# Float64 weights narrowed on VectorE alone, with a new cost model and table of urgencies

## The chip, the cores and the metric

The kernel runs on one core of a Trainium2 chip. A core has five engines with a queue each: TensorE (PE: matmuls, with PEld for its weight loads), VectorE (DVE), ScalarE (ACT), GpSimd (POOL) and SyncE (SP), which here only issues DMAs. The metric is the device time of one execution in microseconds; lower is better.

## The reference, cut to what matters

```python
# attention, 4 x 8 heads, 576 positions, head size 64
q_d, k_d, v_d = means of 4 neighbouring positions          # 144 positions
out_up = repeat(softmax(q_d k_d^T / 8) v_d, 4)              # global part
scores = where(|i - j| < 4, q k^T / 8, -1e9)                # local part, a band
x = out_up + softmax(scores) v                              # -> [2304, 512]
# first feed-forward layer, weights are float64
x = ((x @ w_a) * (x @ w_b)) @ w_out                         # 512 -> 1536 -> 512
# second one, weights are float64, alpha float32
h = x @ w_in
return (max(h, 0) + alpha * min(h, 0)) @ w_out2             # 512 -> 2048 -> 512
```

The five weight matrices come as float64. The kernel reads each number as two 32-bit words and must make a float32 of them (its exponent scaled by a power of two) before it can be used.

## The kernel before, in words

All large products run on TensorE in float16, with each operand split into a high and a low half (`split`, line 413), so that a product is three matmuls. The work has these stages, and the names in the trace are those of the tiles:

- *Attention of batch b* (four batches, six tiles of 96 positions each). `turn` transposes q and k, `soft` makes the band's softmax, `p_turn` and `av_t` multiply with v; the global part is made by `g_top`, `g_minus`, `g_exp`, `g_out` and `od_turn`; `x_add` (line 703) adds the two and splits the sum into `xt`. `v_sum` (line 758) adds neighbouring rows of v on GpSimd, for batches 1 to 3.
- *Weights.* A piece is 1024 numbers a partition (`w_a`, `w_b`, `w_in2`) or 512 (`w_out`, `w_out2`). `narrow` (line 463) turns the two words of a number into one: ScalarE scales the low word into place, VectorE masks sign and top exponent bit as int16, VectorE shifts and masks the high word as int32, and GpSimd adds the two. Then ScalarE takes the sum of squares, and ScalarE and VectorE split the piece into two float16 halves. `wab_chunk`, `wo_words`, `wi_chunk` and `wo2_words` (lines 940 to 1006) call it, for 12, 12, 8 and 16 pieces. The raw pieces lie in a few buffers that are used in turn: the load of a later piece waits until `narrow` and what follows has read the buffer.
- *Main matmuls.* `s1(j, f)` makes 128 columns of the first hidden layer for 288 tokens (j = 0 to 7, f = 0 to 11; 24 matmuls, then two operations each on ScalarE and VectorE); `s2` multiplies with `w_out` and leaves `x2`; `s3` and `s4` are the second layer for blocks of 384 tokens. Blocks j = 0 and 1 are taken together, two f at a time, so that they follow the weights as these are narrowed; then s2 of block 0, s1 of block 2, and so on.

The order of the work is not written by hand. Every instruction goes through a planner (`Plan`, line 26): `cost` (line 93) gives its duration, `lat` (line 186) the delay from an engine to the next, and `reschedule` (line 201) plays the program through, always taking on each engine the ready operation with the highest priority. A priority is the length of work that follows, plus a bias, plus an urgency from the table `URGENT` (line 1259) that has an entry for each group of operations. The main matmuls are a chain whose order is fixed (`chain`, line 440): the planner may put other work between them but not swap them. `fill` (line 244) then puts matmuls on `idf`, which compute nothing, into the gaps that the plan leaves on TensorE between 4 and 200 us. The orders of the queues that come out are fixed in the program; on the chip each engine runs its queue in order and waits on semaphores.

Of the kernel before, what the change touches and what calls it, by code (L numbers as in the profile page):

```python
# [7 lines left out]
F32 = mybir.dt.float32  # L8
F16 = mybir.dt.float16
BF16 = mybir.dt.bfloat16  # L10
# [9 lines left out]

class Op:
    __slots__ = ("eng", "calls", "dur", "bias", "preds", "succ", "tail", "est", "left", "start", "end", "name", "dma",
                 "reads", "writes", "n", "free", "prio")


class Plan:
# [4 lines left out]
    def __init__(self, nc):  # L31
        self.nc = nc
        self.ops = []
        self.group = None
        self.live = {}
        self.bias = 0.0
        self.name = ""
        self.rel = 0.0

    @staticmethod  # L40
    def region(ap):
# [49 lines left out]
        return n  # L91

    def cost(self, eng, method, out, ins, kw):
        n = self.free(out)
        if eng == self.PE:
            if method == "transpose":
                n = self.free(out)
                w = 2 if ins[0].dtype == F32 else 1
            else:
                w = 4 if ins[0].dtype == F32 else 1  # L100
            return max(0.03, n * w * 0.000425)
        m = max([n] + [self.free(a) for a in ins])
        if eng == self.POOL:
            return 0.2 + m * (0.0026 if method == "tensor_tensor" else 0.0011)
        if eng == self.ACT:
            if ins and ins[0].dtype == U32:
                return 0.2 + 0.00095 * m
            return 0.2 + 0.0009 * m + (0.19 if kw.get("accum_out") is not None else 0)
        if out.dtype == I16:
            return 0.1 + 0.00144 * m  # L110
        if method in ("tensor_scalar", "tensor_copy", "memset", "tensor_scalar_mul"):
            return 0.12 + 0.0009 * m
        return 0.14 + 0.0011 * m

    def __call__(self, eng, method, *args, **kw):
        if "out" in kw:
            writes, ins = [kw["out"]], [a for a in args if hasattr(a, "ap")]
        else:
            writes, ins = [args[0]], [a for a in args[1:] if hasattr(a, "ap")]
        out = writes[0]  # L120
        for k, a in kw.items():
            if k == "accum_out":
                if a is not None:
                    writes.append(a)
            elif k != "out" and hasattr(a, "ap"):
                ins.append(a)
        o = self.group
        if o is None or eng != self.PE:
            o = self.new(eng)
        if eng == self.SP:  # L130
            el = kw["in_"]
            parts = [int(c) for _, c in el.ap]
            nb = SIZE[el.dtype]
            for c in parts:
                nb *= c
            run = min(min(int(x.ap[-1][1]) for x in (kw["out"], kw["in_"])) * SIZE[el.dtype], 4096)
            rate = 230e3 if run >= 1024 else 150e3
            o.dma = (nb / rate, 2.2)
            o.dur += 1.0
        else:  # L140
            o.dur += self.cost(eng, method, out, ins, kw)
# [13 lines left out]

    def new(self, eng):
        o = Op()
        o.eng, o.calls, o.dur, o.bias, o.name, o.dma = eng, [], 0.0, self.bias, self.name, None
        o.reads, o.writes, o.preds, o.succ, o.free = [], [], set(), [], self.rel
        return o  # L160

# [22 lines left out]
        o.reads = o.writes = None  # L184

    def lat(self, a, b):
        if a.eng == b.eng and not a.dma:
            return 0.0 if a.eng == self.PE else 0.06
        if a.eng == self.PE:
            return 0.3  # L190
        return 0.2

    def schedule(self, chain):
        for a, b in zip(chain, chain[1:]):
# [74 lines left out]
    def issue(self):  # L269
        for o in self.order:  # L270
            for f, args, kw in o.calls:
                f(*args, **kw)  # L272


LAST = None

# [2 lines left out]
def kernel(  # L279
# [136 lines left out]

    idf = const.tile([128, 128], F32, name="idf")
    ones = const.tile([2, 128], F32, name="ones")

    def top_of(m, n):  # L420

# [38 lines left out]
            return t[:, i + 1].rearrange("p a b c -> p (a b c)").bitcast(F32)  # L460
        return t[:, i + 1].rearrange("p a b -> p (a b)").bitcast(F32)

    def narrow(raw, dst):


        w = raw.bitcast(I32).rearrange("p (n t) -> p n t", t=2)
        h = raw.bitcast(I16).rearrange("p (n t) -> p n t", t=4)
        A("activation", out=w[:, :, 0], in_=raw.bitcast(U32).rearrange("p (n t) -> p n t", t=2)[:, :, 0],
          func=ACTF.Copy, scale=2.0 ** -29)
        V("tensor_scalar", out=h[:, :, 1], in0=h[:, :, 3], scalar1=-0x4000, scalar2=None, op0=ALU.bitwise_and)  # L470
        d = dst.bitcast(I32)
        V("tensor_scalar", out=d, in0=w[:, :, 1], scalar1=3, scalar2=0x3FFFFFFF,
          op0=ALU.logical_shift_left, op1=ALU.bitwise_and)
        G("tensor_tensor", out=d, in0=d, in1=w[:, :, 0], op=ALU.add)

    def cols_in(raw, w, c):
        dma(raw.rearrange("p (k f) -> p k f", k=KD), w[:, c * CW:(c + 1) * CW].rearrange("(k p) f -> p k f", p=128))
# [14 lines left out]
    def rows_in(i, w, raw):  # L492
        dma(raw, w[i * 128:(i + 1) * 128, :])

    def rows_narrow(t, i, n, raw):
        narrow(raw, slot(t, i))
        A("activation", out=raw.bitcast(BF16)[:, :DM], in_=slot(t, i), func=ACTF.Square, accum_out=row_ss[n][:, i:i + 1])

    def split_rows(t, i, rf):
# [12 lines left out]
              op=ALU.mult)  # L512
        return prep_rows(F1, fac, us_o)

    def cols_words(t, i, raw):
        narrow(raw, slot(t, i))

    def cols_bound(t, i0, c):
        m = c["m"] = ring("wm", [128, 2])
# [420 lines left out]
    def wab_chunk(c):  # L940
        st = {}
        for j in range(2):
            cols_words(wab, 2 * c + j, raws[(2 * c + j) % 3])
            wab_load(2 * c + j + 3)
        cols_bound(wab, 2 * c, st)
        cols_split(wab, 2 * c, us_ab, st)
# [7 lines left out]
        rows_in(i, w_out, wo_raw[i])  # L954

    def wo_words(i):
        rows_narrow(wo, i, F1, wo_raw[i])
        for n in {0: [5], 1: [6], 2: [7], 5: [8], 6: [9], 8: [10], 9: [11]}.get(i, []):
            wo_load(n)

# [31 lines left out]
    def wi_chunk(c):  # L992
        x = {}
        for j in range(2):
            cols_words(wi, 2 * c + j, raws2[(2 * c + j) % 4])
            wi_load(2 * c + j + 4)
        cols_bound(wi, 2 * c, x)
        cols_split(wi, 2 * c, us_i, x)
# [3 lines left out]
            rows_in(i, w_out2, xr2[i % 2])  # L1002

    def wo2_words(i):
        rows_narrow(wo2, i, F2, xr2[i % 2])
        wo2_load(i + 2)

    def wo2_fac():
# [5 lines left out]
        V("scalar_tensor_tensor", out=uu, in0=us_o, scalar=2.0 ** 83, in1=us_o2, op0=ALU.mult, op1=ALU.mult)  # L1014

    def unscale(j):
        nt = NB // 128
# [230 lines left out]
    def group(name):  # L1248
# [5 lines left out]
        if name[:3] in ("s1_", "s2_"):  # L1254
# [1 line left out]
        return kind if kind in ("wow", "wos", "wo2w", "wo2s") else name  # L1256


    URGENT = {"alphas": 5, "bs0": 90, "bs1": -15, "bs2": -25, "bs3": 15, "gexp0": -80, "gexp1": -35,
# [12 lines left out]

    cal.sort(key=lambda x: x[:2])
    for _, _, fn, P.name, bias, P.rel in cal:
        P.bias = bias + URGENT.get(group(P.name), 0.0)
        fn()
    P.schedule(chain)
    ib = idf.bitcast(BF16)
# [33 lines left out]
```

## Time and profile before

| | us |
|---|---|
| median of 3 runs | 1025.32 |
| lowest and highest of them | 1024.84, 1025.57 |
| profiled execution, span from first to last instruction | 1025.4 |
| ScalarE busy in that span (46%) | 470.6 |
| TensorE weight loads (beside the matmuls) | 686.7 |

The profile was taken in one execution. An engine's busy time counts the instructions that it works on, waiting aside; a share of busy time over the whole span is a mean over stages with different limits, which is why the rows below are taken by stretches of the span. DMAs moved 69.5 MB, at a mean of 68 GB/s. All instructions carry line 272, which is the planner's `issue`; they are told apart by the tiles that they write and read.

### The profile page before, as it was taken

Reading aid. Unit: us, or ns where it says so; the run is one execution under the profiler, and the core shown is the slowest. Engines: PE = TensorE matmul, PEld = TensorE weight load, DVE = VectorE, ACT = ScalarE, POOL = GpSimd, SP = SyncE. Lnnn points to the kernel's source line nnn. Section 1 sums busy time; section 2 is a strip of 40 time slices with the busy share of each in tenths; the row PEclk is TensorE's granted clock in tenths of the full one; section 3 lists DMA queues with packets and bytes.
Section 4 is the critical chain, followed back from the end, with each engine's and each line's share of the span. In section 5 each row is a group of like instructions: output and inputs, shape, how many; then the busy total and the mean of one; then the engine's idle time right before and its main releaser. Section 6 shows DMA issues by size and latency. Waiting matters only on the chain.

```text
span 1025.4 us, 18493 instructions
## 1 busy us (share of the span) xinstructions
PE 993.8 (97%) x7565; PEld 686.7 (67%) x7565; DVE 610.9 (60%) x1245; ACT 470.6 (46%) x967; POOL 139.8 (14%) x128
## 2 busy tenths in 40 slices
PE   7887899999999999999999999999999999999998
PEld 5666677768878778877777777655545555464553
DVE  6999998857655687566999677431504215152240
ACT  3634487543433344254656646542705336162350
POOL 3445631001200020001244220000000000000000
PEclk9989799989999999999999999999999999999999
DMA  9683451014310053223173311010010100100000
GB/s 208 200 252 106 139 136 42 1 25 76 82 49 1 1 121 85 66 74 115 45 228 109 117 42 48 1 42 21 10 43 12 42 21 9 67 11 11 21 1 31
DMA packets 95941, 69.49 MB, mean 68 GB/s; under 512 B 71152, under 2 KB 78704, under 8 KB 95856
## 3 DMA queue, kind: packets, MB, share of 16 engines
q1 hardware_dynamic: 95856, 68.31, 24.5%
q8 instruction: 59, 0.97, 0.4%
q14 instruction: 26, 0.21, 0.1%
HBM read 58.86 MB, written 9.44 MB: 67 GB/s over the span
## 4 chain that ended last, share of the span: by engine, by line
PE 88%; DVE 9%; issue 1%; DMA 0%; ACT 0%; POOL 0%; SPq 0%; DVEq 0%; POOLq 0%; ACTq 0%
PE m L272 78%; PE a L272 9%; DVE zone L272 2%; DVE wo L272 2%; DVE wab L272 1%; PE r L272 1%; DVE xt L272 1%; DVE gt L272 1%; DVE x2s L272 0%; DVE nm L272 0%; DVE gm L272 0%; DMA zone<-in_v_dram 0%; DVE vst L272 0%; DVE nz L272 0%; DVE gn L272 0%
## 5 line engine op out<-in xcount | busy, mean ns | idle before, releaser
L272 PEld LDWEIGHTS <-wab 128*128 128x128 f16 x3168 | 308.9, 98 | 168.1 <-issue 9.1
L272 PE MATMUL m<-xt,wab 128*128 128x288 f16 x2304 | 299.6, 288 | 8.0 <-DVE xt L272 4.9
L272 PE MATMUL m<-xt,zone 128*128 128x384 f16 x1152 | 188.2, 326 | 0.0
L272 PE MATMUL m<-zone,wab 128*128 128x512 f16 x864 | 187.7, 379 | 0.0
L272 DVE SCALAR_TENSOR_TENSOR gt<-tm,nal,tm 128x384 f32<-128x384 f32 x96 | 59.3, 618 | 208.1 <-ACT tm L272 208.1
L272 PEld LDWEIGHTS <-zone 128*128 128x128 f16 x1152 | 112.7, 98 | 74.9
L272 ACT ACTIVATE tm<-m 128x384 f32<-128x384 f32 (+1 forms) x224 | 97.3, 476 | 104.5 <-PE m L272 104.5
L272 PEld LDWEIGHTS <-wo 128*128 128x128 f16 x1152 | 111.6, 98 | 30.7 <-issue 2.0
L272 POOL TENSOR_TENSOR zone<-zone 72x256 f32<-72x256 f32 (+2 forms) x60 | 78.5, 1318 | 374.4 <-DVE zone L272 135.2
L272 PE MATMUL m<-gt,wo 128*128 128x288 f16 x864 | 111.8, 288 | 0.9 <-DVE x2s L272 0.9
L272 ACT ACTIVATE gt<-m,uf 128x512 f32<-128x512 f32 x18 | 12.4, 687 | 155.6 <-PE m L272 155.6
L272 PE MATMUL a<-zone 64*96 64x104 f32 (+4 forms) x1104 | 76.0, 271 | 3.4 <-DVE zone L272 3.2
L272 ACT ACTIVATE zone<-zone 96x832 f32<-96x832 f32 (+5 forms) x73 | 61.5, 847 | 38.9 <-DVE zone L272 28.2
L272 ACT COPY zone<-a 104x384 f32<-104x384 f32 (+4 forms) x124 | 53.2, 470 | 53.6 <-PE a L272 49.4
L272 PEld LDWEIGHTS a<-zone 64*96 64x96 f32 (+4 forms) x1104 | 60.9, 153 | 21.3 <-issue 13.4
L272 DVE SCALAR_TENSOR_TENSOR tm<-m,tm 128x288 f32<-128x288 f32 x96 | 43.4, 453 | 49.8 <-PE m L272 40.0
L272 ACT COPY tm<-m 128x288 f32<-128x288 f32 x96 | 38.0, 396 | 76.3 <-PE m L272 73.1
L272 DVE SCALAR_TENSOR_TENSOR wab<-gt,kap,wab 128x384 f16<-128x384 f32 x96 | 58.9, 613 | 6.5 <-ACT wab L272 6.5
L272 ACT ACTIVATE wab<-gt,kap 128x384 f16<-128x384 f32 x96 | 59.2, 616 | 1.1 <-DVE gt L272 1.1
L272 ACT ACTIVATE gt<-tm 128x288 f16<-128x288 f32 x72 | 31.8, 443 | 38.9 <-DVE tm L272 38.6
L272 PE MATMUL a<-idf,zone 96*104 96x96 f32 (+4 forms) x392 | 43.7, 252 | 4.6 <-DVE zone L272 2.9
L272 POOL TENSOR_TENSOR wab<-wab,wo 128x1024 int32<-128x1024 int32 x12 | 37.7, 3148 | 58.2 <-DVE wo L272 31.0
(172 smaller groups left out, 920.6 us busy)
## 6 DMA issues: line engine op xcount, KB each, us to landing
zone<-in_moe_w_in_dram SPq DMA_DIRECT2D x8, 1024.0 KB
zone<-in_moe_w_out_dram SPq DMA_DIRECT2D x16, 512.0 KB
wo<-in_moe_w_a_dram SPq DMA_DIRECT2D x6, 1024.0 KB
wo<-in_moe_w_b_dram SPq DMA_DIRECT2D x6, 1024.0 KB
x_d<-x2s SPq DMA_DIRECT2D x8, 576.0 KB
out_dram<-gt SPq DMA_DIRECT2D x18, 256.0 KB
zone<-in_k_dram SPq DMA_DIRECT2D x21, 208.0 KB
zone<-in_v_dram SPq DMA_DIRECT2D x21, 208.0 KB
```

Of the source, the lines that this page charges most:

```text
L272: f(*args, **kw)
```

## The change

`narrow` gets a parameter `way`; the table `WAY` is all zeros, so every call takes the first branch. In that branch VectorE shifts and masks the high word into place, a second operation of VectorE takes sign and top exponent bit from the high word and ors them in, and a third shifts the low word right and ors it in. ScalarE's conversion, the int16 mask and GpSimd's add are not issued. (The second branch is not used. A constant tile `floor` is written once, for that branch.) The planner's `cost` returns a duration and a lag, with other formulas, `lat` uses the lag, and `URGENT` is replaced by a larger table, which now has entries for single `s3` and `s4` groups. `fill` is as before, and works on the new plan.

```diff
     def cost(self, eng, method, out, ins, kw):
         n = self.free(out)
         if eng == self.PE:
-            if method == "transpose":
-                n = self.free(out)
-                w = 2 if ins[0].dtype == F32 else 1
-            else:
-                w = 4 if ins[0].dtype == F32 else 1
-            return max(0.03, n * w * 0.000425)
+            if ins[0].dtype != F32:
+                return max(0.03, n / 2400 + 0.0025), 0.2
             if method == "transpose":
+                return n / 1200 + 0.002, 0.2
+            st = list(ins[0].ap)
+            half = int(st[0][1]) <= 64 or self.free(ins[0]) <= 64
+            return max(n / (1200 if half else 600) + 0.002, 0.13 if int(st[0][1]) > 2 else 0.3), 0.2
...
         if eng == self.POOL:
-            return 0.2 + m * (0.0026 if method == "tensor_tensor" else 0.0011)
+            return 0.15 + m * (0.0023 if method == "tensor_tensor" else 0.0008), 0.03
...
-        if out.dtype == I16:
-            return 0.1 + 0.00144 * m
-        if method in ("tensor_scalar", "tensor_copy", "memset", "tensor_scalar_mul"):
-            return 0.12 + 0.0009 * m
-        return 0.14 + 0.0011 * m
+        if method == "memset":
+            d = 0.06 + 0.00104 * m
+        elif out.dtype == I32 and method == "tensor_tensor":
+            d = 0.16 + 0.0013 * m
+        elif out.dtype == I16:
+            d = 0.2 + 0.00108 * m
+        elif method in ("tensor_scalar", "tensor_copy", "tensor_scalar_mul", "tensor_scalar_add", "tensor_scalar_max"):
+            d = 0.145 + (0.00104 if ps else 0.00052) * m + (0.06 if ptr else 0)
+        else:
+            d = 0.145 + 0.00104 * m + (0.06 if ptr else 0)
+        return d - 0.08, 0.08
...
     def lat(self, a, b):
-        if a.eng == b.eng and not a.dma:
-            return 0.0 if a.eng == self.PE else 0.06
-        if a.eng == self.PE:
-            return 0.3
-        return 0.2
+        if a.eng == b.eng == self.PE:
+            return 0.0
+        return a.lag + (0.2 if a.eng == self.SP else 0.035)
...
+WAY = (0,0,0,0,0)
...
-    def narrow(raw, dst):
-        w = raw.bitcast(I32).rearrange("p (n t) -> p n t", t=2)
-        h = raw.bitcast(I16).rearrange("p (n t) -> p n t", t=4)
-        A("activation", out=w[:, :, 0], in_=raw.bitcast(U32).rearrange("p (n t) -> p n t", t=2)[:, :, 0],
-          func=ACTF.Copy, scale=2.0 ** -29)
-        V("tensor_scalar", out=h[:, :, 1], in0=h[:, :, 3], scalar1=-0x4000, scalar2=None, op0=ALU.bitwise_and)
-        d = dst.bitcast(I32)
-        V("tensor_scalar", out=d, in0=w[:, :, 1], scalar1=3, scalar2=0x3FFFFFFF,
-          op0=ALU.logical_shift_left, op1=ALU.bitwise_and)
-        G("tensor_tensor", out=d, in0=d, in1=w[:, :, 0], op=ALU.add)
+    def narrow(raw, dst, way):
+        d = dst.bitcast(I32)
+        w = raw.bitcast(I32).rearrange("p (n t) -> p n t", t=2)
+        u = raw.bitcast(U32).rearrange("p (n t) -> p n t", t=2)
+        if not way:
+            V("tensor_scalar", out=d, in0=w[:, :, 1], scalar1=3, scalar2=0x3FFFFFFF,
+              op0=ALU.logical_shift_left, op1=ALU.bitwise_and)
+            V("scalar_tensor_tensor", out=d, in0=w[:, :, 1], scalar=-0x40000000, in1=d, op0=ALU.bitwise_and,
+              op1=ALU.bitwise_or)
+            V("scalar_tensor_tensor", out=dst.bitcast(U32), in0=u[:, :, 0], scalar=29, in1=dst.bitcast(U32),
+              op0=ALU.logical_shift_right, op1=ALU.bitwise_or)
+            return
...
-            cols_words(wab, 2 * c + j, raws[(2 * c + j) % 3])
+            cols_words(wab, 2 * c + j, raws[(2 * c + j) % 3], WAY[j])
...
-    URGENT = {"alphas": 5, "bs0": 90, "bs1": -15, "bs2": -25, "bs3": 15, "gexp0": -80, "gexp1": -35,
+URGENT = {"": -180, "alphas": -80, "bs0": -40, "bs1": 120, "bs2": 35, "bs3": 140, "gexp0": -20, "gexp1": -130,
...
```

## Rows read from the trace of the kernel before

**Rows 1.** The page: busy time of engines, and the chain by engine.

```profile
...
PE 993.8 (97%) x7565; PEld 686.7 (67%) x7565; DVE 610.9 (60%) x1245; ACT 470.6 (46%) x967; POOL 139.8 (14%) x128
...
PE 88%; DVE 9%; issue 1%; DMA 0%; ACT 0%; POOL 0%; SPq 0%; DVEq 0%; POOLq 0%; ACTq 0%
```

**Rows 2.** Stretches: length, each engine's busy us (count), PEclk, DMA share, GB/s.

```profile
...
25.00:125.00 100.00, 82.60 (x750) 64.92 (x749) 96.35 (x153) 48.08 (x79) 50.77 (x25) 0.88 0.61 181
125.00:210.00 85.00, 84.75 (x805) 67.64 (x802) 72.64 (x174) 59.98 (x128) 14.48 (x12) 1.00 0.24 58
210.00:246.00 36.00, 34.34 (x318) 26.59 (x315) 23.70 (x64) 14.02 (x28) 1.35 (x2) 0.91 0.31 52
246.00:513.00 267.00, 265.29 (x2463) 211.27 (x2462) 182.97 (x404) 114.40 (x246) 30.44 (x27) 1.00 0.25 63
513.00:1025.00 512.00, 508.38 (x3105) 303.60 (x3104) 219.76 (x420) 224.15 (x471) 35.05 (x20) 1.00 0.14 44
```

**Rows 3.** TensorE's groups, 25:125: count | busy us, mean ns | idle before.

```profile
...
L272 PE MATMUL m<-idf 128*128 128x256 bf16 x280 | 36.6, 283 | 0.0
L272 PE MATMUL m<-xt,wab 128*128 128x288 f16 x86 | 15.3, 350 | 6.8 <-DVE xt L272 4.9 <-ACT xt L272 1.8
```

**Rows 4.** VectorE's groups, 25:125, columns as in rows 3.

```profile
...
L272 DVE TENSOR_SCALAR wo<-wo 128x1024 int16<-128x1024 int16 x12 | 19.0, 1586 | 0.0
L272 DVE TENSOR_SCALAR wab<-wo 128x1024 int32<-128x1024 int32 x12 | 12.2, 1024 | 0.0
L272 DVE TENSOR_TENSOR zone<-zone 128x384 f32<-128x384 f32 x5 | 8.0, 1615 | 0.0
L272 DVE TENSOR_TENSOR zone<-zone,nz 96x832 f32<-96x832 f32 x4 | 7.3, 1816 | 0.0
...
L272 DVE SCALAR_TENSOR_TENSOR wab<-wab,ws 128x1024 f16<-128x1024 f32 x4 | 5.1, 1268 | 0.0
...
L272 DVE SCALAR_TENSOR_TENSOR xt<-xt,sx,xt 128x384 f16<-128x384 f32 x1 | 2.6, 2574 | 0.0
...
L272 DVE TENSOR_SCALAR gn<-gm 72x8 bf16<-72x8 f32 x2 | 2.1, 1078 | 0.0
L272 DVE TENSOR_SCALAR ws<-us_ab 128x2 int32<-128x2 int32 x2 | 1.9, 972 | 0.0
```

**Rows 5.** VectorE's groups, 250:500, columns as in rows 3.

```profile
...
L272 DVE TENSOR_TENSOR zone<-zone,nz 96x832 f32<-96x832 f32 x12 | 12.5, 1038 | 0.2
...
L272 DVE TENSOR_SCALAR zone<-zone 128x1024 int16<-128x1024 int16 x5 | 6.6, 1319 | 1.1 <-ACT zone L272 1.1
...
L272 DVE TENSOR_SCALAR nz<-nz 96x8 f32<-96x8 f32 x11 | 2.4, 215 | 0.1
...
L272 DVE TENSOR_SCALAR zone<-zone 128x1024 int32<-128x1024 int32 x3 | 2.1, 697 | 0.0
...
L272 DVE SCALAR_TENSOR_TENSOR xt<-xt,sx,xt 128x384 f16<-128x384 f32 x1 | 0.6, 612 | 0.0
...
L272 DVE TENSOR_TENSOR xt<-xt,zone 128x384 f32<-128x384 f32 x1 | 0.5, 549 | 0.0
```

**Rows 6.** Timeline of VectorE, 100:119: start us, us, instruction.

```profile
...
108.63 5.91 DVE L272 TENSOR_TENSOR zone<-zone 128x384 f32<-128x384 f32 x1
```

**Rows 7.** Timeline of GpSimd, 100:119.

```profile
...
108.12 1.17 POOL L272 TENSOR_TENSOR zone<-zone 72x256 f32<-72x256 f32 x1
109.26 2.53 POOL L272 TENSOR_TENSOR wo<-wo,x2s 128x512 int32<-128x512 int32 x2
111.75 2.38 POOL L272 TENSOR_TENSOR wab<-wab,wo 128x1024 int32<-128x1024 int32 x1
```

**Rows 8.** GpSimd's groups, 25:125, columns as in rows 3.

```profile
...
L272 POOL TENSOR_TENSOR wab<-wab,wo 128x1024 int32<-128x1024 int32 x12 | 37.7, 3148 | 58.2 <-DVE wo L272 31.0 <-DVE nz L272 10.3 <-issue 7.3
L272 POOL TENSOR_TENSOR zone<-zone 72x256 f32<-72x256 f32 x9 | 9.1, 1022 | 0.2
L272 POOL TENSOR_TENSOR wo<-wo,x2s 128x512 int32<-128x512 int32 x3 | 4.0, 1354 | 3.1 <-DVE x2s L272 3.1
```

More of the change, by code (lines that the diff above doesn't have):

```diff
@@ L22 @@
     __slots__ = ("eng", "calls", "dur", "bias", "preds", "succ", "tail", "est", "left", "start", "end", "name", "dma",
-                 "reads", "writes", "n", "free", "prio")
+                 "reads", "writes", "n", "free", "prio", "lag", "grp")
 class Plan:
@@ L38, in __init__ @@
         self.rel = 0.0
+        self.grp = ""
     @staticmethod
@@ L95, in cost @@
         if eng == self.PE:
+            if ins[0].dtype != F32:
+                return max(0.03, n / 2400 + 0.0025), 0.2
             if method == "transpose":
-                n = self.free(out)
-                w = 2 if ins[0].dtype == F32 else 1
-            else:
-                w = 4 if ins[0].dtype == F32 else 1
-            return max(0.03, n * w * 0.000425)
+                return n / 1200 + 0.002, 0.2
+            st = list(ins[0].ap)
+            half = int(st[0][1]) <= 64 or self.free(ins[0]) <= 64
+            return max(n / (1200 if half else 600) + 0.002, 0.13 if int(st[0][1]) > 2 else 0.3), 0.2
         m = max([n] + [self.free(a) for a in ins])
+        ps = any(str(a.space).endswith("PSUM") for a in ins)
+        ptr = any(self.free(a) == 1 for a in ins) and m > 1
+        step = lambda a: abs(int(list(a.ap)[-1][0])) > 1 and int(list(a.ap)[-1][1]) > 1
         if eng == self.POOL:
-            return 0.2 + m * (0.0026 if method == "tensor_tensor" else 0.0011)
+            return 0.15 + m * (0.0023 if method == "tensor_tensor" else 0.0008), 0.03
         if eng == self.ACT:
-            if ins and ins[0].dtype == U32:
-                return 0.2 + 0.00095 * m
-            return 0.2 + 0.0009 * m + (0.19 if kw.get("accum_out") is not None else 0)
-        if out.dtype == I16:
-            return 0.1 + 0.00144 * m
-        if method in ("tensor_scalar", "tensor_copy", "memset", "tensor_scalar_mul"):
-            return 0.12 + 0.0009 * m
-        return 0.14 + 0.0011 * m
+            d = (0.14 if ps else 0.186) + 0.00084 * m + (0.093 if ptr else 0) + (0.19 if kw.get("accum_out") is not None else 0)
+            if step(out):
+                d += 0.1
+            return d - 0.095, 0.095
+        if method == "memset":
[9 more added lines that the diff above has]
+        return d - 0.08, 0.08
     def __call__(self, eng, method, *args, **kw):
@@ L140, in __call__ @@
         else:
-            o.dur += self.cost(eng, method, out, ins, kw)
+            d, o.lag = self.cost(eng, method, out, ins, kw)
+            o.dur += d
         for a in ins:
@@ L157, in new @@
         o = Op()
-        o.eng, o.calls, o.dur, o.bias, o.name, o.dma = eng, [], 0.0, self.bias, self.name, None
+        o.eng, o.calls, o.dur, o.bias, o.name, o.dma, o.lag = eng, [], 0.0, self.bias, self.name, None, 0.0
+        o.grp = self.grp
         o.reads, o.writes, o.preds, o.succ, o.free = [], [], set(), [], self.rel
@@ L418 @@
     ones = const.tile([2, 128], F32, name="ones")
+    floor = const.tile([128, 1], F32, name="floor")
     def top_of(m, n):
@@ L461, in slot @@
         return t[:, i + 1].rearrange("p a b -> p (a b)").bitcast(F32)
-    def narrow(raw, dst):
+    def narrow(raw, dst, way):
+        d = dst.bitcast(I32)
         w = raw.bitcast(I32).rearrange("p (n t) -> p n t", t=2)
-        h = raw.bitcast(I16).rearrange("p (n t) -> p n t", t=4)
-        A("activation", out=w[:, :, 0], in_=raw.bitcast(U32).rearrange("p (n t) -> p n t", t=2)[:, :, 0],
-          func=ACTF.Copy, scale=2.0 ** -29)
-        V("tensor_scalar", out=h[:, :, 1], in0=h[:, :, 3], scalar1=-0x4000, scalar2=None, op0=ALU.bitwise_and)
-        d = dst.bitcast(I32)
-        V("tensor_scalar", out=d, in0=w[:, :, 1], scalar1=3, scalar2=0x3FFFFFFF,
-          op0=ALU.logical_shift_left, op1=ALU.bitwise_and)
-        G("tensor_tensor", out=d, in0=d, in1=w[:, :, 0], op=ALU.add)
+        u = raw.bitcast(U32).rearrange("p (n t) -> p n t", t=2)
[7 more added lines that the diff above has]
+            return
+        h = raw.bitcast(BF16).rearrange("p (n t) -> p n t", t=4)
+        A("activation", out=w[:, :, 0], in_=u[:, :, 0], func=ACTF.Relu, scale=2.0 ** -29, bias=floor)
+        A("activation", out=dst, in_=h[:, :, 3], func=ACTF.Sign)
+        V("scalar_tensor_tensor", out=w[:, :, 1], in0=w[:, :, 1], scalar=3, in1=w[:, :, 0], op0=ALU.logical_shift_left,
+          op1=ALU.bitwise_or)
+        V("tensor_tensor", out=d, in0=d, in1=w[:, :, 1], op=ALU.add)
     def cols_in(raw, w, c):
@@ L493, in rows_in, with rows_narrow @@
         dma(raw, w[i * 128:(i + 1) * 128, :])
-    def rows_narrow(t, i, n, raw):
-        narrow(raw, slot(t, i))
+    def rows_narrow(t, i, n, raw, way):
+        narrow(raw, slot(t, i), way)
         A("activation", out=raw.bitcast(BF16)[:, :DM], in_=slot(t, i), func=ACTF.Square, accum_out=row_ss[n][:, i:i + 1])
@@ L513, in emit_wo_prep, with cols_words @@
         return prep_rows(F1, fac, us_o)
-    def cols_words(t, i, raw):
-        narrow(raw, slot(t, i))
+    def cols_words(t, i, raw, way):
+        narrow(raw, slot(t, i), way)
     def cols_bound(t, i0, c):
@@ L581, in setup1 @@
         G("memset", ones, 1.0)
+        G("memset", floor, -0.501)
         pm = pool_m[:, :, 48:48 + TP]
@@ L956, in wo_words @@
     def wo_words(i):
-        rows_narrow(wo, i, F1, wo_raw[i])
+        rows_narrow(wo, i, F1, wo_raw[i], WAY[2])
         for n in {0: [5], 1: [6], 2: [7], 5: [8], 6: [9], 8: [10], 9: [11]}.get(i, []):
@@ L994, in wi_chunk @@
         for j in range(2):
-            cols_words(wi, 2 * c + j, raws2[(2 * c + j) % 4])
+            cols_words(wi, 2 * c + j, raws2[(2 * c + j) % 4], WAY[3])
             wi_load(2 * c + j + 4)
@@ L1004, in wo2_words @@
     def wo2_words(i):
-        rows_narrow(wo2, i, F2, xr2[i % 2])
+        rows_narrow(wo2, i, F2, xr2[i % 2], WAY[4])
         wo2_load(i + 2)
@@ L1013, in wo2_fac @@
         late["rf"] = prep_rows(F2, fac2, us_o2)
-        V("scalar_tensor_tensor", out=uu, in0=us_o, scalar=2.0 ** 83, in1=us_o2, op0=ALU.mult, op1=ALU.mult)
+        V("scalar_tensor_tensor", out=uu, in0=us_o, scalar=2.0 ** (83 + sum(WAY)), in1=us_o2, op0=ALU.mult, op1=ALU.mult)
     def unscale(j):
@@ L1256, in group @@
         return kind if kind in ("wow", "wos", "wo2w", "wo2s") else name
-    URGENT = {"alphas": 5, "bs0": 90, "bs1": -15, "bs2": -25, "bs3": 15, "gexp0": -80, "gexp1": -35,
[12 rows of a table removed]
     cal.sort(key=lambda x: x[:2])
     for _, _, fn, P.name, bias, P.rel in cal:
-        P.bias = bias + URGENT.get(group(P.name), 0.0)
+        P.grp = group(P.name)
+        P.bias = bias + URGENT.get(P.grp, 0.0)
         fn()
```

38 rows, old and new, of the table URGENT are left out of this document.

## The prediction

> **What bounds the kernel now.** Read the page's busy line first: TensorE is busy 993.8 us of 1025.4, VectorE 610.9, GpSimd 139.8 [rows 1]. Taken whole, that says TensorE is the bound and nothing done to the weights can matter. The table of stretches says where that is not so [rows 2]. From 246 us on TensorE is full (265.3 of 267, then 508.4 of 512) at granted clock 1.00, with VectorE at 183.0 and 219.8 us: no work saved on VectorE there shortens anything. Between 25 and 125 us it is the other way round: VectorE is busy 96.35 of 100 us, and TensorE, for all its 82.6 busy us, has little to do. The groups of TensorE in that stretch show it [rows 3]: 36.6 us are the 280 fill matmuls on `idf`, which compute nothing, and only 86 matmuls (15.3 us) are main work (`xt`, `wab`), which waited for VectorE's and ScalarE's `xt`. So the head is bound by VectorE: it narrows the weights, does the softmax of the first batch and scales `x`, all in one queue whose order the planner wrote. The chain that ended last gives VectorE 9% of the span [rows 1], about 92 us, and most of that must lie in the head, as TensorE is hardly idle later. Between 125 and 210 us TensorE is full (84.75 of 85) with VectorE at 72.6; from 210 to 246 us it loses a little (34.3 of 36, clock 0.91).
>
> The second thing to see is why VectorE is so full. Compare its groups between 25 and 125 us [rows 4] with the same kinds of instruction between 250 and 500 us [rows 5], when GpSimd does little: a 128x384 add took 1615 ns against 549, a 96x832 multiply 1816 against 1038, the int32 shift 1024 against 697, the int16 mask 1586 against 1319, the 128x384 scale-and-subtract of `xt` 2574 against 612. One add took 5.91 us, from 108.63 us on [rows 6]; in that time GpSimd ran its own adds without a break (from 109.26 us two `wo` adds of 2.53 us together, between others) [rows 7]. So VectorE stands still while GpSimd adds. On GpSimd the stretch has twelve adds of weights (37.7 us), three of `wo` (4.0 us) and nine of the `v` sums (9.1 us) [rows 8].
>
> **The change, part by part.**
>
> *GpSimd's adds go.* What VectorE gets back in the head is head mean less quiet mean, times count [rows 4, 5]: int32 12 x 0.327 = 3.9; int16 12 x 0.267 = 3.2; adds 5 x 1.066 = 5.3; multiplies 4 x 0.778 = 3.1; the `xt` scale 2.0; and four operations on a few elements (two of 1078 ns, two of 972 ns, against 215 ns for such a one) 1.7 + 1.5 = 3.2. Sum 20.7 us. The `v` sums stay, and they are 9.1 of GpSimd's 50.8 us, so I take 82% of it: -17.0 us. All of it is on VectorE, which has only 3.65 us of idle time in that stretch, so I count it on the path.
>
> *Narrowing itself.* Per piece of 1024 words VectorE did an int16 mask and an int32 shift, 1.319 + 0.697 = 2.02 us when undisturbed [rows 5]. It will do the shift and two two-input operations (and-or, shift-or) on int32. The trace has no such operation. Lower end: each costs what the one-input int32 shift costs, 0.697, which makes +0.08 us a piece. Upper end: each costs as much as the strided int16 mask in the head, 1.586, which makes +1.85. I take the nearest in shape, the two-input operation on 1024 elements that splits a weight, 1.268 [rows 4]: 0.697 + 2 x 1.268 = 3.23, which is +1.22 a piece. Twelve pieces: +14.6 us (0.9 to 22.2). Three pieces of `wo` at half the size: +1.8 us (0.1 to 2.8).
>
> The rows that speak against this exchange are those of the 96x832 multiply: it has two inputs in SBUF and was held up, 1816 ns against 1038 [rows 4, 5], and both new operations have two as well. [...]
>
> VectorE in the head therefore comes out at -17.0 + 14.6 + 1.8 = -0.6 us, with ends at -20.7 + 1.0 = -19.7 and +25.0 (all of the new work, none of the relief on the path). It is an exchange: a stall that the planner could not see for work that it can.
>
> *ScalarE's conversion goes.* ScalarE is busy 48.1 us of these 100 [rows 2] and not the bound: 0. Bounds: -3.65 us (all of VectorE's idle time in the stretch, should ScalarE be behind it) and 0. *Loads of weights*: the raw buffer now comes free with VectorE's third operation, not GpSimd's add, so SP's loads issue a little earlier; DMA engines are at 0.61 there: 0. `w_in2` and `w_out2` are narrowed behind 246 us, under a full TensorE, and the rest of `w_out` under the full stretch from 125 to 210 us: 0. Without that cover the 24 later pieces would cost 8 x 1.22 + 16 x 0.61 = 20 us, but VectorE has 84 us idle from 246 to 513 us and 292 after that. One more `memset` on GpSimd at the start: under 0.1 us.
>
> *Clock.* [...] Waits of 2 to 3 us behind a stalled VectorE become rarer, not extinct: I take half, -4 (0 to -8.6).
>
> *Cost model and urgencies.* The order of every queue is written anew. The order of main matmuls is fixed by the chain, so only what is put between them, and VectorE's and ScalarE's order, can move. What a better order can win is time in which VectorE is idle before the main work of batch 1 at 246 us: 3.65 + 12.4 + 12.3 = 28.4 us after 25 us [rows 2]. In the middle part (12.4) TensorE was full, so it can be won only by having main work earlier. What a worse order can cost I bound by the 6.8 us that main matmuls waited in the head [rows 3], twice over: +14. I take -8, between these ends and nearer to nothing than to -28, because the old order was written without the stalls in it (its cost for a 128x384 add is 0.14 + 0.0011 x 384 = 0.56 us, where the head took 1.615 [rows 4]) and the new one meets a machine that is closer to its plan.
>
> Sum: -0.6 - 4 - 8 = -12.6. The profiled execution has a span of 1025.4 us and the median of the runs is 1025.32, so nothing lies around the span that has to be added: 1013 us.
>
> **Rivals.** (1) *The head packs.* Main matmuls start earlier and never stop: order -20 (two thirds of the 28.4), clock -8.6, VectorE -5 (a quarter of its lower end): 992 us. For it: 36.6 us of fill and 17.4 us of idle TensorE in the head; against it: VectorE cannot be more than full. (2) *An even exchange.* Only the -0.6 comes, and order and clock give nothing: 1025. (3) *Slower: VectorE's load decides.* Place: the twelve pieces in the head. If the stalls lay mostly where VectorE would have waited anyway, the added 14.6 + 1.8 us stay and nothing is given back: 1025.4 + 16.4 = 1042 us. It decides as soon as a piece costs VectorE over 2.02 + 17.0/12 = 3.4 us, or the same price with less relief. For it: VectorE is the full engine, and the change puts work from two half-idle engines onto it. Against it: the longest stall, 5.91 us, stands on an add to `x`, from which `xt` is made, and `xt` is what main matmuls waited for [rows 3, 6]. (4) *The `v` sums take over the stalls.* The 24 new operations with two inputs are held as the multiply was. Each of nine sums of 1.02 us [rows 8] would hold VectorE or be held: +9.2 us, 1022.
>
> **How the numbers follow.** Forecast 1013: 0.42, its own range 1004 to 1022. Packed head (992): 0.16. `v` sums (1022): 0.10. Even exchange (1025): 0.09. VectorE's load (1042, from 1028 on): 0.23. A run of this kernel cannot tell 0.2% (2.1 us) from no change. Faster: 0.42 + 0.16 + 0.10 = 0.68; same 0.09; slower 0.23. For 8 in 10 I leave out the lower half of the packed head and the upper half of the slow case: 996 to 1034.
>
> **What will show it.** Right: GpSimd's adds on weights gone; in the head a 128x384 add near 550 ns and no VectorE instruction over 3 us; two new operations near 1.27 us on 1024 words; between 25 and 125 us fewer fill matmuls than 280 and more main ones than 86; nothing changed from 513 us on but when it starts. Wrong: the two-input integer operations well over 1.27 us; VectorE still full to 125 us and main matmuls no earlier; new idle time of TensorE between 246 and 1025 us, which would say that the table, not the narrowing, set the time.

## The result, and the profile after

The changed kernel takes 1002.91 us (median of 4 runs, 1002.11 to 1003.87) against 1025.44 us beside it: a ratio of 0.9775, with a 95% interval of 0.976 to 0.979. That is 22.5 us less, where 12.6 were forecast: 1002.9 lies just below the forecast's own range of 1004 to 1022 us and inside the 996 to 1034 to which it gave 8 chances in 10. The profiled execution has a span of 1002.1 us. Beside the runs below, the kernel before took 1025.4 to 1027.1 us, so differences of 1 to 2 us between runs are not read.

The page of the changed kernel, busy time of engines and the chain by engine:

```profile
...
PE 977.7 (98%) x7488; PEld 672.5 (67%) x7488; DVE 608.3 (61%) x1293; ACT 434.4 (43%) x919; POOL 39.5 (4%) x81
...
PE 84%; DVE 13%; issue 1%; ACT 1%; DMA 0%; POOL 0%; DVEq 0%; POOLq 0%
```

Against [rows 1], GpSimd went from 139.8 to 39.5 us and ScalarE from 470.6 to 434.4; VectorE's total is the same, 608.3 against 610.9. The chain that ended last is on VectorE for 13% of the span, where it was 9%: the kernel has become shorter although more of its path is VectorE's.

Stretches of the changed kernel (columns as in rows 2):

```profile
...
25.00:125.00 100.00, 89.84 (x878) 69.23 (x879) 97.18 (x191) 45.17 (x89) 13.62 (x12) 0.98 0.63 178
125.00:210.00 85.00, 82.45 (x786) 64.24 (x784) 79.32 (x207) 51.99 (x109) 0.00 (x0) 0.98 0.27 71
210.00:246.00 36.00, 36.00 (x348) 29.00 (x346) 24.20 (x47) 15.21 (x33) 8.81 (x12) 1.00 0.52 96
246.00:513.00 267.00, 267.00 (x2443) 212.66 (x2440) 189.62 (x417) 109.24 (x242) 9.26 (x12) 1.00 0.28 77
513.00:1025.00 512.00, 485.30 (x2919) 285.34 (x2916) 203.04 (x402) 202.93 (x429) 0.00 (x0) 1.00 0.10 32
```

Read them against [rows 2]. From 25 to 125 us (the head) VectorE is as full as before (97.2 us of 100), the granted clock is 0.98 instead of 0.88, and TensorE is busy 89.8 us, where it was 82.6. The next lines say with what. TensorE's groups in that stretch:

```profile
...
L285 PE MATMUL m<-xt,wab 128*128 128x288 f16 x204 | 26.3, 286 | 2.1 <-DVE xt L285 2.1
L285 PE MATMUL m<-idf 128*128 128x256 bf16 x203 | 26.3, 274 | 0.0
```

204 main matmuls instead of 86, at 286 ns instead of 350, and 203 fill matmuls instead of 280 [rows 3]. The timeline of TensorE shows where the 118 come from; first the kernel before, then the changed one (start us, us, count; only main matmuls are copied):

```profile
...
78.81 0.29 PE L272 MATMUL m<-xt,wab 128*128 128x288 f16 x1
81.50 7.59 PE L272 MATMUL m<-xt,wab 128*128 128x288 f16 x47 [2.40 <-DVE xt L272]
...
115.24 0.28 PE L272 MATMUL m<-xt,wab 128*128 128x288 f16 x1 [1.85 <-ACT xt L272]
118.03 4.24 PE L272 MATMUL m<-xt,wab 128*128 128x288 f16 x17 [2.51 <-DVE xt L272]
```

```profile
...
82.58 0.29 PE L285 MATMUL m<-xt,wab 128*128 128x288 f16 x1
84.07 5.92 PE L285 MATMUL m<-xt,wab 128*128 128x288 f16 x47 [1.21 <-DVE xt L285]
...
98.19 0.29 PE L285 MATMUL m<-xt,wab 128*128 128x288 f16 x1
99.33 5.92 PE L285 MATMUL m<-xt,wab 128*128 128x288 f16 x47 [0.85 <-DVE xt L285]
```

The first main matmul is not earlier but 3.8 us later. What has gone is the hole behind the first block of 48: main work stood still from 89.1 to 115.2 us before, and from 90.0 to 98.2 after.

VectorE's groups from 25 to 125 us (columns as in rows 3):

```profile
...
L285 DVE SCALAR_TENSOR_TENSOR wab<-wo,wab 128x1024 int32<-128x1024 int32 x12 | 14.5, 1210 | 0.0
L285 DVE SCALAR_TENSOR_TENSOR wab<-wo,wab 128x1024 uint32<-128x1024 uint32 x12 | 14.5, 1209 | 0.0
L285 DVE TENSOR_SCALAR wab<-wo 128x1024 int32<-128x1024 int32 x12 | 8.5, 711 | 0.0
L285 DVE SCALAR_TENSOR_TENSOR wab<-wab,ws 128x1024 f16<-128x1024 f32 x6 | 7.7, 1287 | 0.0
...
L285 DVE TENSOR_TENSOR zone<-zone,nz 96x832 f32<-96x832 f32 x5 | 5.1, 1028 | 0.0
...
L285 DVE TENSOR_TENSOR zone<-zone 128x384 f32<-128x384 f32 x5 | 2.7, 543 | 0.0
...
L285 DVE SCALAR_TENSOR_TENSOR xt<-xt,sx,xt 128x384 f16<-128x384 f32 x1 | 0.6, 599 | 0.0
```

The stalls of [rows 4] are gone: the 128x384 add takes 543 ns (1615 before), the 96x832 multiply 1028 (1816), the `xt` scale 599 (2574). In their place stand 24 two-input operations of 1.21 us. GpSimd in that stretch has only the `v` sums, 12 instead of the 9 in [rows 8], with the same count|time columns:

```profile
...
L285 POOL TENSOR_TENSOR zone<-zone 72x256 f32<-72x256 f32 x12 | 13.6, 1148 | 93.9 <-DVE tr L285 64.4 <-DMA zone<-in_v_dram 29.3
```

### The profile page after: what moved, and what is told of

The parts are those of the page before. It is cut to its first block, busy times and chain, and to the rows that moved or that the text cites. A ratio compares the mean times of both kernels' runs of the same rounds, so it can differ in the third digit from the quotient of the medians.

```text
span 1002.1 us, 18185 instructions
## 1 busy us (share of the span) xinstructions
PE 977.7 (98%) x7488; PEld 672.5 (67%) x7488; DVE 608.3 (61%) x1293; ACT 434.4 (43%) x919; POOL 39.5 (4%) x81
## 4 chain that ended last, share of the span: by engine, by line
PE 84%; DVE 13%; issue 1%; ACT 1%; DMA 0%; POOL 0%; DVEq 0%; POOLq 0%
PE m L285 75%; PE a L285 8%; DVE wab L285 4%; DVE zone L285 3%; DVE wo L285 2%; DVE nz L285 1%; DVE gt L285 1%; PE r L285 1%; DVE nm L285 1%; DVE tm L285 0%; DVE xt L285 0%; DMA zone<-in_v_dram 0%; DVE vst L285 0%; ACT wo L285 0%; ACT wab L285 0%
## 5 line engine op out<-in xcount | busy, mean ns | idle before, releaser
L285 PE MATMUL m<-xt,wab 128*128 128x288 f16 x2304 | 296.2, 286 | 2.5 <-DVE xt L285 2.1
L285 PE MATMUL a<-zone 64*96 64x104 f32 (+4 forms) x1104 | 72.8, 265 | 0.6 <-DVE zone L285 0.5
L285 PEld LDWEIGHTS a<-zone 64*96 64x96 f32 (+4 forms) x1104 | 58.4, 149 | 19.9 <-issue 14.6
L285 ACT ACTIVATE zone<-zone 96x832 f32<-96x832 f32 (+3 forms) x49 | 41.9, 855 | 51.8 <-DVE zone L285 49.0
L285 ACT COPY tm<-m 128x288 f32<-128x288 f32 x96 | 37.8, 394 | 43.1 <-PE m L285 40.7
L285 PE MATMUL a<-idf,zone 96*104 96x96 f32 (+4 forms) x392 | 41.6, 247 | 3.8 <-DVE sx L285 1.9
L285 POOL TENSOR_TENSOR zone<-zone 72x256 f32<-72x256 f32 x36 | 31.7, 893 | 307.9 <-DMA zone<-in_v_dram 167.2
L285 DVE SCALAR_TENSOR_TENSOR zone<-zone 128x512 int32<-128x512 int32 (+3 forms) x48 | 40.8, 861 | 0.4
```

## The experiments

Theory A was the prediction's: on VectorE stalls and new work cancel, and order and clock make the gain. Theory B: the stalls behind GpSimd's adds were what kept the head long. Rival C: VectorE's load decides, and only the new order saved the change.

**The two halves apart.** `e1_narrow_alone` has the new `narrow`, with `cost`, `lat` and `URGENT` of before; `e2_plan_alone` has the new ones of these and the old `narrow`.

```diff
 # e1, against the changed kernel            # e2, against the changed kernel
-    new cost(), lat(), URGENT                -    new narrow()
+    those of the kernel before               +    that of the kernel before
```

> The new narrowing alone: three operations of VectorE, with the old cost model and the old table of urgencies, and the order planned from these. Theory A (the exchange on VectorE is even, and the rest of the gain is order and clock): 1018 to 1025 us. Theory B (the stalls behind GpSimd's adds were what kept the head long, so that taking them away is most of the gain): 1003 to 1012. Rival C (VectorE's load decides, and only the new order saved the change): 1033 to 1042.

> The new cost model and table alone, with the old narrowing (ScalarE, VectorE twice, GpSimd's add), planned anew. Theory A: 1010 to 1017, order and part of the clock without the exchange. Theory B: 1018 to 1030, as the stalls that the plan does not know of undo what it gains. A theory that the table is everything: 1000 to 1006.

Measured: e1 1017.1 us (ratio 0.991, 0.989 to 0.992), e2 1032.1 us (1.006, 1.004 to 1.007). e1 lies just under A's 1018 to 1025, and outside B's and C's ranges. e2 lies just over B's 1018 to 1030 and far from A's range and that of the table alone: the new plan with the old narrowing is *slower* than the kernel before, by 0.6%. So the gain is not a sum: -8.3 and +6.7 against 1025.4 give -22.5 together.

**GpSimd's adds, cut to one word, in both plans.** `e4_adds_cut` is the kernel before and `e13_plan_alone_cut` is e2, with every instruction in its place. All 48 adds of narrowing are cut; fifteen of them stand in the head of the kernel before [rows 8].

```diff
     P.schedule(chain)
+    for o in P.order:
+        f, a, kw = o.calls[0]
+        if o.eng == "gpsimd" and kw.get("op") == ALU.add and kw["out"].dtype == I32:
+            o.calls = [(f, a, dict(kw, out=kw["out"][:, :1], in0=kw["in0"][:, :1], in1=kw["in1"][:, :1]))]
```

> The kernel before with every instruction in its order, and each of GpSimd's 48 adds of narrowing cut to one word a partition: the other words keep no low word and no sign, which is left out. Only the stalls and the length of the adds go. A and B: 17 to 21 us of VectorE's time in the head come back, of which the order can use most: 1004 to 1012. C: 1022 to 1026.

> As e2_plan_alone (1032 us), every instruction in its order, with GpSimd's adds of narrowing cut to one word a partition; the other words keep no low word and no sign, which is left out. If stalls behind these adds are what made the new plan slow with the old narrowing: 988 to 1003. If the new table does not suit the old narrowing for another reason: 1015 to 1030.

Measured: e4 997.8 us (0.973, 0.970 to 0.975), e13 1003.0 us (0.978, 0.975 to 0.980): 27.6 us less than the kernel before, 29.1 less than e2. Both are past the gain that A and B had for e4. Cutting an add takes away two things, the time for which VectorE stands still beside it and the time that a piece waits for the add itself. As the order of VectorE's queue is the same, the traces tell them apart: here are VectorE's first 187 and first 423 instructions, in the kernel before and then in e4 (columns as in rows 2).

```profile
...
0.00:125.00 125.00, 101.01 (x884) 77.61 (x885) 111.86 (x187) 58.06 (x97) 58.52 (x69) 0.90 0.69 186
0.00:246.00 246.00, 220.10 (x1999) 171.83 (x2000) 208.21 (x423) 132.06 (x251) 74.35 (x82) 0.94 0.48 122
```

```profile
...
0.00:100.40 100.40, 92.16 (x906) 71.90 (x907) 87.83 (x187) 58.74 (x99) 33.70 (x69) 1.00 0.88 229
0.00:217.50 217.50, 207.41 (x1999) 163.29 (x2000) 181.88 (x423) 131.41 (x251) 38.58 (x81) 0.99 0.56 138
```

The same 187 instructions take 24.0 us less of VectorE's busy time and are done 24.6 us earlier; the same 423 take 26.3 us less and are done 28.5 us earlier. VectorE's idle time hardly changes (13.1 and 12.6 us, then 37.8 and 35.6). So nearly all that the adds cost is VectorE standing still, as B said; their own length and all else have about 2 us. In e13 the first 426 instructions take 26.5 us less than in e2. Medians in a table:

| narrowing | old model and table | new model and table |
|---|---|---|
| old | 1025.4 | 1032.1 |
| old, adds cut, same order | 997.8 | 1003.0 |
| new | 1017.1 | 1002.9 |

Down the first two rows: the adds cost 28 to 29 us in both plans. Across: with the old narrowing the new plan is worth nothing, with the adds (+6.7) or with them cut (+5.2); with the new one it is worth -14.2. VectorE's groups in e4, 25 to 125 us:

```profile
...
L272 DVE TENSOR_SCALAR wo<-wo 128x1024 int16<-128x1024 int16 x12 | 15.7, 1310 | 0.0
L272 DVE TENSOR_SCALAR wab<-wo 128x1024 int32<-128x1024 int32 x12 | 8.1, 682 | 0.0
...
L272 DVE TENSOR_TENSOR zone<-zone,nz 96x832 f32<-96x832 f32 x5 | 5.6, 1120 | 0.0
...
L272 DVE TENSOR_TENSOR zone<-zone 128x384 f32<-128x384 f32 x5 | 2.6, 539 | 0.0
```

The same instructions in the same order as [rows 4], near the durations of [rows 5]: 1310 ns against 1319, 682 against 697, 539 against 549, and 1120 against 1038 for the multiply; in that stretch GpSimd still has twelve `v` sums, 12.9 us in all. In e2, where the adds are whole, instructions are held up again, though not all the same ones; the rows of the 96x832 multiply, of the five 128x384 adds and of the first 128x384 add to `x`:

```profile
...
L285 DVE TENSOR_TENSOR zone<-zone,nz 96x832 f32<-96x832 f32 x4 | 7.3, 1824 | 0.0
...
L285 DVE TENSOR_TENSOR zone<-zone 128x384 f32<-128x384 f32 x5 | 2.6, 547 | 0.0
...
L285 DVE TENSOR_TENSOR xt<-xt,zone 128x384 f32<-128x384 f32 x1 | 2.1, 2091 | 0.0
```

1824 ns against 1120 in e4, and 2091 against 549 in [rows 5], but 547 for the five that took 1615 in the kernel before. The planner gives a fixed duration to each instruction, so it cannot know of these.

**Which part of the plan.** `e5_old_table` is the changed kernel with the old table; model and narrowing are the new ones.

```diff
-URGENT = {"": -180, "alphas": -80, ...
+URGENT = {"alphas": 5, "bs0": 90, ...
```

> The new narrowing and the new cost model with the old table of urgencies, planned anew; beside it stand 1017.1 us for the new narrowing with the old model and table, and 1002.9 for all three. If the table is what turns free time of VectorE into earlier matmuls: 1012 to 1022. If the cost model does it: 1003 to 1008.

Measured: 1016.8 us (0.992, 0.989 to 0.994). With the old table the new model changes nothing (1017.1 in e1); on the new model the table makes the 14 us. The new table on the old model was not run. Where the time goes, the stretches say; first e5, then the changed kernel:

```profile
...
300.00:360.00 60.00, 57.51 (x528) 45.09 (x527) 37.17 (x91) 22.48 (x50) 0.00 (x0) 0.97 0.03 11
360.00:420.00 60.00, 55.36 (x503) 43.47 (x501) 37.83 (x80) 23.79 (x51) 7.93 (x10) 0.94 0.41 86
```

```profile
...
300.00:360.00 60.00, 60.00 (x533) 47.72 (x530) 42.12 (x96) 23.88 (x54) 7.84 (x10) 1.00 0.29 57
360.00:420.00 60.00, 60.00 (x565) 48.17 (x562) 34.68 (x75) 22.03 (x49) 0.00 (x0) 1.00 0.24 60
```

e5 loses 2.5 and 4.6 us of TensorE's time and runs at clock 0.97 and 0.94; the changed kernel loses none. What TensorE waited for there in e5:

```profile
...
351.27 0.38 PE L285 MATMUL r<-tr,ones 1*128 1x1 f32 x2 [1.69 <-DVE tr L285]
...
370.20 0.37 PE L285 MATMUL r<-idf,xm 128*1 128x128 f32 x1 [3.87 <-DVE xm L285]
```

These are transposes and broadcasts that find a scale: the first that of a batch's `x` (`batch_scale`), the second that of `x2` (`x2_out`). With the old table VectorE reaches them late. In e5 it is not the head, there e5 is ahead, with 240 main matmuls where the changed kernel has 204:

```profile
...
L285 PE MATMUL m<-xt,wab 128*128 128x288 f16 x240 | 30.7, 286 | 2.8 <-DVE wab L285 1.4 <-DVE xt L285 1.3
```

In e1, which has the old model as well, the loss lies elsewhere: between 300 and 420 us TensorE loses 0.7 us, but between 125 and 210 us 9.6 us at clock 0.94, where the changed kernel loses 2.6 at 0.98.

```profile
...
125.00:210.00 85.00, 75.45 (x676) 56.91 (x675) 75.92 (x189) 52.61 (x110) 0.00 (x0) 0.94 0.25 67
```

So the old table loses about the same 14 us in either plan, in different places.

**VectorE's load in the head.** `e8_and_or_twice` issues one operation twice, `e10_no_low_word` leaves one out (and plans anew).

```diff
 # e8, after P.schedule(chain): the and-or of the 12 large pieces of the first layer
+            o.calls = o.calls * 2
 # e10, in narrow()
-            V("scalar_tensor_tensor", out=dst.bitcast(U32), in0=u[:, :, 0], scalar=29, in1=dst.bitcast(U32),
-              op0=ALU.logical_shift_right, op1=ALU.bitwise_or)
```

> The changed kernel with every instruction in its order, and the and-or of VectorE issued twice for each of the twelve large pieces of the first layer (the second time changes nothing in the result): 12 x 1.21 = 14.5 us more on VectorE, and nothing on another engine. If the head is still VectorE's (B, and rival C in its mild form): 1013 to 1019. If VectorE now has slack there: 1003 to 1007.

> The changed kernel without the third operation of narrowing, planned anew: the low word's three bits are left out, so a weight keeps 20 bits behind its leading one. VectorE has 12 x 1.21 = 14.5 us less to do in the head and is at what two operations took before. If the head is VectorE's, us for us: 987 to 991. If the order cannot use it: 998 to 1003.

Measured: e8 1019.5 us (0.995, 0.993 to 0.996), +16.6 for 14.5 us more; e10 994.5 us (0.970, 0.967 to 0.972), -8.4 for 14.5 us less. The head is still VectorE's: more work costs at least its own length, less gives back 0.6 of it, short of the 987 to 991 expected. Stretch 25 to 125 us of e8 and of e10:

```profile
...
25.00:125.00 100.00, 80.49 (x725) 61.01 (x725) 96.80 (x176) 35.38 (x65) 12.29 (x9) 0.90 0.54 156
```

```profile
...
25.00:125.00 100.00, 89.47 (x879) 68.27 (x881) 93.68 (x198) 48.00 (x97) 14.91 (x12) 0.98 0.72 200
```

In e8 TensorE is busy 9 us less than in the changed kernel and the clock falls to 0.90, which is where the 2 us beyond 14.5 may come from. e10, which leaves out the low word's bits, is faster than both kernels. Another table for it, looked for with the planner, added nothing (`e12_new_table`):

```diff
-URGENT = {"": -180, "alphas": -80, "bs0": -40, ...
+URGENT = {"": 60, "alphas": 70, ...   # and the third operation left out, as in e10
```

> e10_no_low_word (994.5 us; the low word's three bits are left out) with another table of urgencies, looked for with the planner for this narrowing. A table made for the other narrowing should leave a little: 989 to 993. If there is nothing left in the order: 994 to 997.

Measured: 996.1 us (0.971, 0.969 to 0.972), not apart from e10.

**The clock.** `e9_no_fill`:

```diff
-    P.fill(4.0, 200.0, chain, banks["m"][2], ib[:, :128], ib, 0.112)
```

> The changed kernel without the 232 fill matmuls, all else in its order. If they keep the granted clock up and cost nothing: the clock between 25 and 125 us falls from 0.98 to 0.80 to 0.90 and the time is 1006 to 1014. If they stand in the way of the matmuls that count: 998 to 1001. If they do neither: 1002 to 1004.

Measured: 1011.9 us (0.988, 0.985 to 0.990), 9.0 us more than with fill. Its stretch from 25 to 125 us:

```profile
...
25.00:125.00 100.00, 75.65 (x581) 56.48 (x582) 88.59 (x176) 41.12 (x77) 10.11 (x11) 0.69 0.61 175
```

The clock is 0.69, lower than expected, where it is 0.98 with fill, and TensorE is busy 75.65 us instead of 89.84. So fill carries the clock in the head, and the 9.0 us are what it is worth here.

**Adds put back.** `e3_adds_beside` and `e11_adds_on_constant` add GpSimd's adds to the changed kernel, behind each piece.

```diff
 # e3
+            g.calls = [(nc.gpsimd.tensor_tensor, (), dict(out=scr[:, :min(205, n - c)], in0=d[:, c:min(c + 205, n)],
+                       in1=d[:, c:min(c + 205, n)], op=ALU.add)) for c in range(0, n, 205)]
 # e11: z is the constant idf
+            g.calls = [(nc.gpsimd.tensor_tensor, (), dict(out=scr[:, :1], in0=d[:, :1], in1=d[:, :1], op=ALU.add))]
+            g.calls += [(nc.gpsimd.tensor_tensor, (), dict(out=scr, in0=z, in1=z, op=ALU.add))] * (P.free(d) // 205)
```

> The changed kernel with every instruction in its order, and beside it, after each narrowed piece, adds on GpSimd over the same words into a scratch tile that nobody reads, five of 205 words for a large piece. Nobody waits for their result; they only compete. If stalls of VectorE behind GpSimd lie on the path of the head (A and B): VectorE stands 10 to 20 us longer between 25 and 125 us and the time is 1012 to 1022. If the stalls fall into slack (C): 1002 to 1006.

> As e3_adds_beside, but the adds on GpSimd read a constant tile: after each narrowed piece one add of one word of it and then four adds of 128 words (two for a small piece) of the constant, so that hardly anyone can wait for GpSimd and what is left is competition. If competition alone cost e3 its 23 us: 1014 to 1024. If it was the wait of later splits for GpSimd's reads: 1003 to 1008.

Measured: e3 1026.2 us (1.001, 0.999 to 1.002), +23.3, more than expected; e11 1010.8 us (0.985, 0.984 to 0.987), +7.9, between its two ranges. Neither is a clean copy of the old stalls. In e11 it is GpSimd's instructions that take longer: its 128-word adds between 25 and 125 us, where VectorE is busy 91.2 us of 100, and then after 513 us, where VectorE of the changed kernel is busy 203.0 us of 512:

```profile
...
L285 POOL TENSOR_TENSOR scr<-idf 128x128 int32<-128x128 int32 x44 | 52.6, 1195 | 3.4
```

```profile
...
L285 POOL TENSOR_TENSOR scr<-idf 128x128 int32<-128x128 int32 x49 | 27.9, 570 | 3.8
```

1195 ns against 570. VectorE's rows in the same stretch of e11 are near those of the changed kernel (1060 ns against 1028, 543 against 543):

```profile
...
L285 DVE TENSOR_TENSOR zone<-zone,nz 96x832 f32<-96x832 f32 x4 | 4.2, 1060 | 0.0
...
L285 DVE TENSOR_TENSOR zone<-zone 128x384 f32<-128x384 f32 x5 | 2.7, 543 | 0.0
```

In e3 the adds took 72 us of GpSimd in the head. Counted by VectorE's instructions as for e4, at 246 us e3 is 18.5 us behind the changed kernel, and VectorE's busy time has 12.8 us of it; e11 is 8.9 us behind, and VectorE's busy time has 3.2. In both, VectorE also waits for a load of `w_out` near 125 us (3.2 and 3.7 us), which it does not in the changed kernel; waits for the added adds themselves come to 1.0 us in e3. The rest, about 2 us each, was not followed. So the adds of 205 words in e3 cost mostly by holding VectorE (12.8 of 18.5 us), those of 128 words of a constant in e11 less so (3.2 of 8.9), and how much the old ones cost is shown by e4 and e13.

**The `v` sums.** `e14_v_sums_cut`, in the changed kernel:

```diff
+        if o.eng == "gpsimd" and kw.get("op") == ALU.add:
+            o.calls = [(f, a, dict(kw, **{x: kw[x][:, :1, :1] for x in ("out", "in0", "in1")}))]
```

> The changed kernel with every instruction in its order, and each of the 36 adds of the v sums on GpSimd cut to one element; the rest of the sums is left out. The rival that the v sums take over the stalls says 993 to 998. If what they still cost is a few stalls of under 1 us, mostly where VectorE has time: 1000 to 1003.

Measured: 1001.3 us (0.976, 0.974 to 0.978): 1.6 us under the changed kernel, with intervals that overlap: no cost of the `v` sums is shown beyond that.

## Why the prediction was right, and where its terms were off

- *VectorE bounds the head, GpSimd's adds hold it up.* Right. The stalls vanish where the adds do (changed kernel, e4), and come back where the adds stay (e2). The two-input 128x384 add took 1615 ns beside the adds and 539 in e4; the one-input int32 shift was held as well, 1024 ns against 682 in e4.
- *The stalls' size.* This is the term that was most off: -17.0 forecast, -27.6 and -29.1 measured (e4, e13). VectorE's busy time itself has nearly all of it: 24.0 us up to the place that was 125 us, 26.3 up to 246 us. The forecast read 20.7 from six kinds of instruction and left out the others that were held, then took 18% off for the `v` sums, though 24.0 came back with the `v` sums still in place; the 2.3 us behind 125 us it counted at nothing.
- *Narrowing itself.* Forecast 3.23 us a piece, measured 0.711 + 1.210 + 1.209 = 3.13: +13.3 us for twelve instead of +14.6, on a basis of 2.02. Right in mechanism and size, and e8 shows that such work costs at least its length here (+16.6 us for 14.5). The two-input integer operations took 1.21 us on 1024 words, where 1.27 was taken from the split of a weight.
- *ScalarE and the loads at 0.* Neither was tried alone. ScalarE lost 36 us of work in all. Main matmuls waited 1.8 us for ScalarE's `xt` before [rows 3] and do not in the changed kernel; but that wait is gone in e4 too, where ScalarE keeps its conversions, so nothing speaks against the 0.
- *Clock.* No run shows the term by itself, -4 of at most 8.6, which was the author's estimate from [rows 2, 3]: 0.12 of 46.0 us in the head and 0.09 of 34.3 us from 210 to 246, the work other than fill. What the runs show is the granted clock, 0.98 in the head instead of 0.88 and 1.00 from 210 to 246 us instead of 0.91 (0.98 from 125 to 210, where it was 1.00). In e4 the clock of the head came to 1.00, and VectorE's busy time accounts for 26.3 of the 28.5 us by which it is ahead at the 423rd instruction. The clock and all else have 2 us there, so that as a term beside the stalls -4 was too much rather than too little. With the clock of the head down from 0.98 to 0.69, as fill is left out, the kernel took 9.0 us more (e9).
- *Cost model and urgencies.* -8 forecast, -14.2 measured on the new narrowing (e1 against the changed kernel), with the table making it on the new model (e5). Too small by 6 us, and the bound was not safe: the forecast counted VectorE's idle time before 246 us alone. In e1 the loss does lie there, from 125 to 246 us; but in e5 the old table opens a hole between 300 and 420 us, where the kernel before lost under 1 us, so an order can lose time behind 246 us too. The reason given, that the new plan meets a machine closer to its plan, is not borne out: with the adds cut, and the stalls gone with them, the new plan on the old narrowing is still 5.2 us slower than the old plan (e13, e4). It gains only together with the new narrowing. That the term had the right sign is in part luck.
- *The sum.* 22.5 for 12.6. One way through the runs: the adds go, -27.6 (e4), where stalls and clock were forecast at -21.0; VectorE does the work instead, with the old model and table, +19.3 (e4 to e1), where +16.4 was forecast; the new plan, -14.2, where -8 was. So the stalls and the order were each too small by over 6 us, and the new work by 3. By another way the steps come out otherwise, as e2 shows. (The forecast put nothing around the span; the changed kernel's profiled execution took 1003.9 us with a span of 1002.1. As a difference of two kernels it cancels.)
- *Signs.* One sign of being wrong came half true: VectorE is still full to 125 us and the first main matmul no earlier. The forecast held all the same, because what VectorE does in that time is more of the work that main matmuls wait for: 204 of them run in it instead of 86.
- *Rivals.* The packed head came half: main work starts no earlier but hardly stops. (Two thirds of 28.4 are 18.9, not 20, so its time should have been 993 and not 992.) The even exchange (1025) fell. The slow case fell as a forecast, yet its price was real: VectorE's added work costs us for us (e8), and e1 shows what it leaves of the stalls' gain without the table, 1017.1 against 997.8. The `v` sums (1022) fell: cutting them gives 1.6 us, not clear of noise (e14).

## What to carry to other kernels

Where GpSimd and VectorE work at the same time, compare VectorE's durations of one instruction shape in a stretch with GpSimd and in one without, before believing that the work was moved to an idle engine for free: here the adds of narrowing, 3 us each in the head, cost the kernel 27.6 us, more than the 19.3 us that their work cost when VectorE, the fullest engine of the head (96.35 us of 100, [rows 2]), did it (e4 to e1). Count such stalls over all of that engine's instructions, not over the kinds that stand out: six kinds gave 20.7 us, the whole queue up to the same instruction 24.0. And judge an order made by a planner together with the change that it comes with: the new plan was 6.7 us slower with the old narrowing and 14.2 us faster with the new one. A new table need not pay, though: for the narrowing without the low word it gave nothing (e12).

## What the runs showed of the hardware that was not expected

Long adds on GpSimd held VectorE; short ones took longer beside it. The weights' adds, of 512 and 1024 words, cost VectorE 24.0 us in the head (e4 against the kernel before). In e11 the 128-word adds took 1195 ns in the head, with VectorE busy 91.2 us of 100, and 570 after 513 us, while VectorE's own durations in the head hardly moved (1060 ns against 1028, 543 against 543). In e4 even an add of a single word could take 1.25 us in the head. Two of them on GpSimd, and below what VectorE did from 48 to 51 us:

```profile
...
34.12 0.19 POOL L272 TENSOR_TENSOR wab<-wab,wo 128x1 int32<-128x1 int32 x1 [2.28 <-DVE wo L272]
...
48.92 1.25 POOL L272 TENSOR_TENSOR wab<-wab,wo 128x1 int32<-128x1 int32 x1 [2.05 <-DVE wgr L272]
```

```profile
...
48.85 1.27 DVE L272 SCALAR_TENSOR_TENSOR wab<-wab,ws 128x1024 f16<-128x1024 f32 x1
50.04 0.19 DVE L272 RECIPROCAL wgs<-wgr 72x8 f32<-72x8 f32 x1
...
```

The second add starts just behind VectorE's two-input split and ends with it, 0.05 us later: it took 1.25 us for what the first did in 0.19. Both are adds of one word of `wab`, so here the moment decided and not the shape. On average the twelve one-word adds of `wab` took 1287 ns in the head of e4, and the six of `wo` with `x2s` 206.
